# A spectral and gated feed-forward layer on one core: turned token tiles that share tables, six loads in two queues, and new orders

## The chip, the cores and the metric

The kernel runs on one core of a Trainium2 chip. The metric is device time in microseconds (us) of one launch; the lower the better. The engines are named as in the profile: PE (TensorE, matmuls; PEld its weight loads), DVE (VectorE), ACT (ScalarE), POOL (GpSimd) and SP (SyncE, which only issues transfers). Each engine works through its own instructions in order and waits on semaphores for the others. Transfers between DRAM and the on-chip memory (SBUF) run on 16 DMA engines that all issuers share.

## The reference

Two steps on x of 2048 tokens by 576 channels, in bf16: a spectral filter of the normalised input, added to x, and then a gated feed-forward of the normalised sum, added again.

```python
def _A_ref(x, w_r, w_i):
    B, S, D = x.shape
    X = jnp.fft.rfft2(x.astype(jnp.float32), axes=(-2, -1))
    X = X * (w_r + 1j * w_i)
    return jnp.fft.irfft2(X, s=(S, D), axes=(-2, -1)).astype(jnp.bfloat16)

def _B_ref(x, w_gate, w_up, w_down):
    return (_gelu(x @ w_gate) * (x @ w_up)) @ w_down

h = x + _A_ref(_layernorm(x), A_w_r, A_w_i)
h2 = h + _B_ref(_layernorm(h), B_w_gate, B_w_up, B_w_down)
```

The inner width of the feed-forward is 4608; the norms have no weights.

## The kernel before

The transforms are done as matmuls with cosine and sine tables. Token s = 16 n1 + n2 stands in partition n1 of tile n2, so x is 16 tiles of 128 by 576 in one buffer `XO`, and a row of SBUF is a run of 16 x 576 numbers in DRAM.

**Loads** (lines 421 to 464). SP issues all of them, in the order of `LORD` (line 25): `x0-2` is tiles 0 and 1 of x, `a0-4` four tiles of the first table `ATB` (cosines and sines of the token transform, 128 by 128 per tile). Then come the tables `FT` and `BT`, 22 pieces of the spectral weights into `WS`, and the tables of the later stages. Every list of rows starts with 128 partitions, or with 16 blocks of rows for the weights.

**A stage** (lines 470 to 560). The order of its work is written out by hand in `SEQ1` (line 24), a word for each step; each engine sees its own words in that order. The tiles go in six groups of 2, 2, 3, 3, 3 and 3 (`GROUPS`). By word:
- `B` c: the statistics of tile c on DVE, two `bn_stats` (line 480). Tiles 3, 4 and 13 have theirs from ACT: `S` c the sum (line 471), `Q` c the sum of squares (line 475).
- `v` i, `q` i, `c` i: variance on DVE, square root on ACT, reciprocal on DVE for group i.
- `x` i: the group's tables times that factor into `ATS`, on POOL (line 505, `P`) or DVE (line 510, `D`).
- `n` i: the negative of the upper half of the channels into `XN`, on POOL (line 552).
- `M` i: the group's matmuls on PE (line 536). Five passes k per group, in the order 1, 3, 4, 0, 2, each in a PSUM bank of its own: four take 128 channels from each half of the 576, in two matmuls per tile; pass 4 takes the 64 channels left over, as two matmuls with 32 columns.
- `E` n and `F` n: the eviction of pass n (five for each group) from PSUM into `U`, by ACT (`A`) or DVE (`D`), line 547; `F` is the second half of a pass whose `E` did the first.
- `k`: matmuls on zeros, which nothing reads.

POOL's instructions wait for one another: each writes the key `_pool` (line 186).

**Middle stages** (lines 601 to 689). 16 frequency blocks i go through D (matmuls over channels, line 606, evicted to `CUS` by ACT), B (line 616, evicted to `YS`), T (product with the weights, DVE, into `TP`, two buffers), Z (sums, DVE), V (line 646) and R (the leftover frequencies), in the order of `SEQF` (line 28). Then come the last transforms, the second norm and the feed-forward (from line 731 on), whose matmuls fill the rest of the run.

**Stores** (line 978). Each of the 16 tiles leaves in two parts, from SP; the last tile is cut at channel 448.

Of the kernel before, what the change touches and what calls it, by code (L numbers as in the profile page):

```python
# [4 lines left out]
BF16 = mybir.dt.bfloat16  # L5
# [7 lines left out]
NZ = 5  # L13
# [10 lines left out]
SEQ1 = """k14 Q3 B1 B0 n0 S3 n2 v0 B2 v1 q0 q1 c0 x0D M0 S4 c1 Q4 B5 B6 E4A E2A v2 B7 q2 n1 E0A E1A x1P c2 k104 M1 B8 x2P B9 E6A n3 v3 E3A E5A E8A q3 k202 M2 B10 B12 E9A n4 E11A E12A S13 c3 B11 E10A E7A v4 x3P M3 B14 q4 c4 E13A E14A x4P B15 Q13 v5 E17A q5 E16A E15D M4 c5 E19A E20A x5D E18D E23A n5 E22D E21D E24A M5 E25A F23D F24A E26A F25D E27A E29A F29A E28D F28D F22A F26D F27A""".split()  # L24
LORD = "x0-2 x2-4 a0-4 x4-8 a4-8 x8-12 x12-16 a8-16".split()
SPLIT = tuple(int(w[1:-1]) for w in SEQ1 if w[0] == "F")
ACT_TILES = tuple(int(w[1:]) for w in SEQ1 if w[0] == "Q")
SEQF = """w0 w1 D0 D1 D2 B0 T0 D3 B1 Z0 T1 B2 D4 T2 D5 Z1 B3 B4 T3 D6 Z2 w2 D7 Z3 B5 V1 V0 T4 T5 Z4 B6 w3 B7 T6 D8 Z5 T7 V2 D9 Z6 B8 T8 V3 Z7 V4 D10 B9 R0 D11 V5 Z8 B10 T9 R1 T10 B11 D12 Z9 V6 D13 Z10 B12 T11 D14 T12 B13 V8 Z11 V7 B14 T13 Z12 D15 Z13 T14 V9 R2 V10 Z14 B15 V13 T15a T15b V11 Z15a V12 Z15b R3 V14 V15 R4""".split()
# [17 lines left out]
def build_tables():  # L46
# [27 lines left out]
    T["ATAB"] = A.reshape(128, 16 * 128)  # L74
    I = I.reshape(128, 16, 128)
    T["ITAB"] = np.stack([I[:, :NPRE], -I[:, :NPRE]], 1).reshape(128, -1)
# [10 lines left out]
    dr = np.concatenate([np.arange(256, 288), np.arange(544, 576)])  # L87
    for o, kk in enumerate((k2o, k2e)):
        for h, fn in enumerate((np.cos, np.sin)):
            for t in range(2):  # L90
                fr[3 * o + t, :, h] = fn(ang(np.arange(128 * t, 128 * t + 128), kk))
            fr[3 * o + 2, 0:64, h] = fn(ang(dr, kk))
# [5 lines left out]
    for st in range(2):  # L98
        g = 1 - st
        for p in range(128):  # L100
# [31 lines left out]
            for zp, t, cf in terms:  # L132
                V[st, zp, p, t, :, sl, 0] = cf.real
                V[st, zp, p, t, :, sl, 1] = cf.imag
    B[:, 2] = -B[:, 0]
# [177 lines left out]
def _build(nc, A_x, A_w_r, A_w_i, B_w_gate, B_w_up, B_w_down, out):  # L313
# [28 lines left out]
    XN = sb.alloc("XN", [128, NT, 288], BF16)  # L342
# [17 lines left out]
    MK = sb.alloc("MK", [128, 4], F32)  # L360
    OS = sb.alloc("OS", [128, 2, D], BF16)
# [23 lines left out]
    ATB = sb.alloc("ATB", [128, NT, 128], BF16)  # L385
# [6 lines left out]
    TP = sb.alloc("TP", [128, 2, 2, 2, KW], BF16)  # L392
# [25 lines left out]
    P.op(POOL, lambda g: g.memset(MK[:, :], 0.0), w=["MK"])  # L418
    for j in range(4):
        P.op(POOL, lambda g, j=j: g.memset(MK[32 * j:32 * j + 32, j:j + 1], 1.0), w=["MK"])  # L420
    xv = A_x[0].rearrange("(p c) d -> p c d", c=NT)
    ov = out[0].rearrange("(p c) d -> p c d", c=NT)
    tabs = dram["ATAB"].rearrange("p (c k) -> p c k", c=NT)

    def x_load(i, c0, c1):
        P.dma(SP, XO[:, c0:c1, 0:D], xv[:, c0:c1, :], f"x{i}", w=[("X", c) for c in range(c0, c1)])

    def atb_load(i, c0, c1):
        P.dma(SP, ATB[:, c0:c1, :], tabs[:, c0:c1, :], f"atb{i}", w=[("ATB", c) for c in range(c0, c1)])

    for i, w in enumerate(LORD):
        (x_load if w[0] == "x" else atb_load)(i, int(w[1:].split("-")[0]), int(w.split("-")[1]))
# [33 lines left out]
    P.op(POOL, lambda g: g.memset(U[64:128, 4, :, :, :], 0.0), w=["Uz"])  # L466
# [11 lines left out]
    def ln1_tile(c):  # L478
        for h in range(2):
            P.op(DVE, lambda v, c=c, h=h: v.bn_stats(ST1[:, c, h, :], XO[:, c, 288 * h:288 * h + 288]), r=[("X", c)], w=[("ST1", c, h)])  # L480

    def ln1_var(i):
        c0, c1 = GROUPS[i]
        for c in range(c0, c1):
            if c in ACT_TILES:
                P.op(DVE, lambda v, c=c: v.tensor_scalar(TM[:, 0, c:c + 1], SA[:, 0, c:c + 1], SA[:, 0, c:c + 1], 1.0 / (D * D), op0=ALU.mult, op1=ALU.mult), r=[("SA0", c)], w=[("TM", c)])
            else:
                P.op(DVE, lambda v, c=c: v.bn_aggr(MV1[:, c, :], ST1[:, c, :, :]), r=[("ST1", c, 0), ("ST1", c, 1)], w=[("MV1", c)])
        for c in range(c0, c1):
            if c in ACT_TILES:  # L490
                P.op(DVE, lambda v, c=c: v.tensor_scalar(MV1[:, c, 1:2], SA[:, 1, c:c + 1], 1.0 / D, TM[:, 0, c:c + 1], op0=ALU.mult, op1=ALU.subtract), r=[("SA1", c), ("TM", c)], w=[("MV1", c)])
# [10 lines left out]
    def ln1_scale(i, eng):  # L502
        c0, c1 = GROUPS[i]
        if eng == POOL:
            P.op(POOL, lambda g, c0=c0, c1=c1: g.tensor_tensor(ATS[:, c0:c1, :], ATB[:, c0:c1, :],
                                                               RS1[:, c0:c1].unsqueeze(2).to_broadcast([128, c1 - c0, 128]), op=ALU.mult),
                 r=[("RS1", i)] + [("ATB", c) for c in range(c0, c1)], w=[("ATS", c) for c in range(c0, c1)])
        else:
            for c in range(c0, c1):
                P.op(DVE, lambda v, c=c: v.tensor_scalar(ATS[:, c, :], ATB[:, c, :], RS1[:, c:c + 1], None, op0=ALU.mult),  # L510
                     r=[("RS1", i), ("ATB", c)], w=[("ATS", c)])
# [11 lines left out]
    def a_mm(i):  # L523
        c0, c1 = GROUPS[i]
        for k in AORD:
            b = a_bank(i, k)
            for c in range(c0, c1):
                o = 128 * (c - c0)
                if k == 4:
                    parts = [(XO[:, c, 256 + 288 * h:288 + 288 * h], 32 * h, 32 * h + 32, True, True) for h in range(2)]  # L530
                else:
                    d0 = 128 * (k // 2)
                    x2 = XN[:, c, d0:d0 + 128] if k % 2 else XO[:, c, 288 + d0:416 + d0]
                    parts = [(XO[:, c, d0:d0 + 128], 0, 128, True, False), (x2, 0, 128, False, True)]
                for lhs, p0, p1, s, e in parts:
                    P.op(PE, lambda t, b=b, lhs=lhs, p0=p0, p1=p1, s=s, e=e, o=o, c=c: t.matmul(bank(b, p0, p1, o, o + 128), lhs, ATS[:, c, :], start=s, stop=e),  # L536
                         r=[("X", c), ("ATS", c)] + ([("XN", c)] if k % 2 else []), w=[("PS", b)])

    def a_ev(n, eng, late=False):
# [4 lines left out]
        m, b, w = c1 - c0, a_bank(i, k), 64 if k == 4 else 128  # L544
        src = bank(b, 0, w, 0, 128 * m).rearrange("p (n g e) -> p n g e", n=m, g=16)[:, :, g0:g1, :]
        dst = U[0:w, k, g0:g1, c0:c1, :].rearrange("p g n e -> p n g e")
# [3 lines left out]
    def x_neg(i):  # L550
        c0, c1 = GROUPS[i]
        P.op(POOL, lambda g: g.tensor_scalar(XN[:, c0:c1, :], XO[:, c0:c1, 288:D], -1.0, 1.0, op0=ALU.mult, op1=ALU.mult),  # L552
             r=[("X", c) for c in range(c0, c1)], w=[("XN", c) for c in range(c0, c1)])

    ENG = {"A": ACT, "D": DVE, "P": POOL}
    RUN1 = {"k": idle_mm, "S": act_sum, "Q": act_sq, "B": ln1_tile, "v": ln1_var, "q": ln1_sqrt, "c": ln1_rs, "M": a_mm, "x": ln1_scale, "E": a_ev, "F": lambda n, eng: a_ev(n, eng, True), "n": x_neg}
# [15 lines left out]
    P.alias([("XN", c) for c in range(NT)], [("V", g, c) for g in range(NG) for c in range(2)])  # L572
    uk = [[("U", i, k, h) for i in range(len(GROUPS)) for h in range(2)] + (["Uz"] if k == 4 else []) for k in range(5)]
# [27 lines left out]
    def st_D(i, eng=ACT):  # L601
        b0, s3 = FB["D", i], i % 3
        for o in range(2):
            b = b0 + o
            for m, us in enumerate((1 - o, 3 - o, 4) if o == 0 else (4, 1 - o, 3 - o)):
                P.op(PE, lambda t, b=b, m=m, us=us, o=o: t.matmul(bank(b, 0, 128, 0, 2 * HK), U[:, us, i, :, :], FT[:, 3 * o + (2 if us == 4 else us // 2), :], start=(m == 0), stop=(m == 2)),  # L606
                    r=[("U", q, us, i // 8) for q in range(len(GROUPS))] + (["Uz"] if us == 4 else []) + ["FT"], w=[("PS", b)])
        ev(eng, CUS[:, s3, :, :].rearrange("p a (j r) -> p a j r", r=2), banks(b0, 2, 2 * HK).rearrange("p r (a j) -> p a j r", a=2),
           [("PS", b0), ("PS", b0 + 1)], [("CU", s3)])
# [10 lines left out]
    def st_T(i, q0=0, q1=KW, hs=(0, 1)):  # L620
        g, sl = GORD[i], i % 2
# [3 lines left out]
        P.op(DVE, lambda v: v.tensor_tensor(TP[:, sl, :, :, q0:q1], y4, w4, op=ALU.mult),  # L625
             r=[("Y", sl), ("Wn", i)] + (wkeys[0] if 1 <= g < 9 else wkeys[1] if g else wkeys[0] + wkeys[1]), w=[("T", sl, h) for h in hs])
# [6 lines left out]
    def st_Z(i, hs=(0, 1)):  # L633
        sl, z3 = i % 2, i % NZ
# [291 lines left out]
    P.alias([("ATB", c) for c in range(NT)], [("AT", f) for f in gu_early])  # L926
# [13 lines left out]
    fdead = ["DT", "IT", "J0", "J1", "ZD"] + [(n_, c) for n_ in ("ATB", "ATS") for c in range(NT)] + [("G", 0, 0), ("G", 0, 1), ("G", 1, 0), ("G", 1, 1), ("Y", 0), ("Y", 1)]  # L940
    fdead += [("T", a, h) for a in range(2) for h in range(2)] + [("Z", a) for a in range(NZ)] + [("ZR", a, h) for a in range(2) for h in range(4)]
# [21 lines left out]
    def down(tb, p):  # L963
# [3 lines left out]
        for h, (d0, d1) in enumerate(((0, cut), (cut, D))):  # L967
# [10 lines left out]
            P.dma(SP, ov[:, c, d0:d1], OS[:, p % 2, d0:d1], f"so{p % 2}{h}", r=[("OS", p % 2, h)], w=[("OUT", p % 2, h)])  # L978
# [65 lines left out]
```

## Time and profile before

Three runs took 491.40, 491.56 and 491.87 us, median 491.56. The profiled execution took 491.75, of which the span from the first to the last instruction is 490.0.

| stretch, us | what | PE busy | DVE busy | ACT busy | POOL busy | DMA share |
|---|---|---|---|---|---|---|
| 0 to 7.67 | first loads, norms of the first tiles | - | from 3.68 | from 4.43 | - | - |
| 7.67 to 20.37 | rest of the A stage | 10.73 of 12.70 | 12.10 | 11.71 | 8.62 | 1.08 |
| 48.60 to 60.00 | last transforms, second norm | 11.24 of 11.40 | 9.04 | 9.24 | 4.66 | 1.01 |

The granted TensorE clock is 1.00 throughout. A DMA share of 1 means that all 16 engines had a packet all the time; it can pass 1 a little where packets overlap.

The loads that the A stage waits for, by issue and landing:

| piece | KB | issued | landed |
|---|---|---|---|
| x0-2 | 288 | 0.73 | 3.66 |
| x2-4 | 288 | 1.19 | 4.41 |
| a0-4 | 128 | 1.65 | 4.71 |
| x4-8 | 576 | 2.12 | 7.67 |
| a4-8 | 128 | 2.59 | 8.55 |
| x8-12 | 576 | 3.07 | 10.31 |
| x12-16 | 576 | 3.54 | 11.77 |
| a8-16 | 256 | 4.01 | 12.45 |

The groups' matmuls start on PE at 7.29 (M0), 10.30, 11.96, 15.04, 16.78 and 18.50 (M5). The profile's table of groups has each of the 26 `bn_stats` at 0.44 (one starts every 0.36), POOL's `XN` of two tiles at 0.67 and of three at 0.91, its scaled tables of two at 0.61 and of three at 0.83, and ACT's evictions of 128 by 384 at 0.47 to 0.49 (one every 0.37).

### The profile page before, as it was taken

How to read it: one execution, taken by the hardware profiler on the slowest of the kernel's cores; microseconds unless marked ns; L12 is line 12 of the kernel's file. 1: busy time of each engine (PE TensorE's matmuls, PEld its weight loads, DVE VectorE, ACT ScalarE, POOL GpSimd, SP SyncE). 2: the span in 40 equal slices, each digit the busy share in tenths (PEclk: the TensorE clock that was granted, in tenths of full speed). 3: DMA queues.
4: the chain of work that ended last, by engine and by line, in shares of the span. 5: the costliest groups of instructions: out<-in, count | busy, mean ns of one | idle time of the engine just before them, and what ended most of it. 6: DMA issues, size and time to landing. Idle time of an engine off the chain costs nothing.

```text
span 490.0 us, 9967 instructions
## 1 busy us (share of the span) xinstructions
PE 482.7 (99%) x4391; PEld 311.6 (64%) x4392; DVE 193.6 (40%) x397; ACT 151.2 (31%) x297; POOL 31.8 (6%) x58
## 2 busy tenths in 40 slices
PE   7999999999999999999999999999999999999998
PEld 3787788888888744444577644444677544444775
DVE  6799733433576634333311144433211233333111
ACT  6999743223322222322200033233100122323000
POOL 6411441000000020000000000000000000000000
DMA  8990999100001071100000001000000000000000
GB/s 284 248 313 6 354 363 351 30 15 2 1 16 37 18 233 23 26 1 1 2 18 16 17 18 23 17 1 0 7 19 19 7 1 0 1 2 1 13 20 18
DMA packets 25148, 31.20 MB, mean 64 GB/s; under 512 B 11440, under 2 KB 17840, under 8 KB 25104
## 3 DMA queue, kind: packets, MB, share of 16 engines
q1 hardware_dynamic: 22208, 18.62, 13.1%
q0 software_dynamic: 2896, 11.95, 7.0%
q8 instruction: 34, 0.56, 0.5%
q14 instruction: 10, 0.08, 0.1%
HBM read 26.22 MB, written 2.36 MB: 58 GB/s over the span
## 4 chain that ended last, share of the span: by engine, by line
PE 94%; DVE 2%; DMA 1%; issue 1%; POOL 0%; ACT 0%; SPq 0%; DVEq 0%; POOLq 0%
PE PS L872 57%; PE PS L973 29%; PE PS L606 2%; PE PS L536 2%; DMA XO<-in_A_x_dram 1%; PE PS L890 1%; PE PS L616 1%; PE PS L731 1%; DVE TP L625 1%; PE PS L774 1%; PE PS L646 1%; PE PS L908 1%; DVE VR L661 0%; DVE ZS L636 0%; POOL XN L552 0%
## 5 line engine op out<-in xcount | busy, mean ns | idle before, releaser
L872 PE MATMUL PS<-HT,WG 64*128 64x512 bf16 (+1 forms) x2160 | 229.0, 371 | 0.1
L872 PEld LDWEIGHTS PS<-HT,WG 64*128 64x128 bf16 x2160 | 130.3, 94 | 96.9 <-issue 1.1
L881 DVE TENSOR_TENSOR AT<-GL,PS 128x512 bf16<-128x512 bf16 (+1 forms) x147 | 99.3, 676 | 178.3 <-ACT GL L880 178.3
L880 ACT ACTIVATE GL<-PS 128x512 bf16<-128x512 f32 (+1 forms) x147 | 86.5, 588 | 262.9 <-PE PS L872 251.6
L973 PE MATMUL PS<-WD,AT 128*128 128x288 bf16 (+2 forms) x1152 | 144.9, 286 | 0.0
L973 PEld LDWEIGHTS PS<-WD,AT 128*128 128x128 bf16 x1152 | 110.7, 98 | 30.6 <-ACT GL L880 0.8
L872 PE MATMUL PS<-HT,WGX 64*128 64x512 bf16 x486 | 53.4, 376 | 0.0
L976 DVE TENSOR_TENSOR OS<-PS,XO 128x288 bf16<-128x288 f32 (+2 forms) x32 | 14.6, 456 | 94.5 <-PE PS L973 94.4
L872 PEld LDWEIGHTS PS<-HT,WGX 64*128 64x128 bf16 x486 | 23.7, 94 | 28.8
L606 PE MATMUL PS<-FT,U 128*128 128x288 bf16 x96 | 13.7, 286 | 0.0
L625 DVE TENSOR_TENSOR TP<-YS,WS 128x1152 bf16<-128x1152 bf16 (+2 forms) x17 | 11.9, 719 | 2.9 <-ACT YS L598 2.6
L536 PE MATMUL PS<-ATS,XO 128*128 128x128 bf16 (+1 forms) x128 | 10.1, 221 | 2.9 <-ACT U L547 1.2
L895 ACT ACTIVATE EB<-PS 128x288 f32<-128x288 f32 x10 | 4.1, 411 | 27.7 <-PE PS L890 27.7
L480 DVE BATCH_NORM_STATS2 ST<-XO 128x6 f32<-128x288 bf16 x26 | 10.0, 438 | 3.9 <-DMA XO<-in_A_x_dram 3.9
L536 PEld LDWEIGHTS PS<-ATS,XO 128*128 128x128 bf16 (+1 forms) x128 | 7.5, 97 | 5.5 <-DVE ATS L510 1.5
L606 PEld LDWEIGHTS PS<-FT,U 128*128 128x128 bf16 x96 | 9.3, 98 | 2.3
L913 DVE TENSOR_TENSOR XO<-PS,XO 128x576 bf16<-128x576 f32 x10 | 7.6, 757 | 8.0 <-PE PS L908 8.0
L598 ACT ACTIVATE CUS<-PS 128x576 bf16<-128x576 f32 x16 | 10.4, 655 | 0.5 <-PE PS L606 0.2
L598 ACT ACTIVATE YS<-PS 128x576 bf16<-128x576 f32 x16 | 10.1, 655 | 0.0
L547 ACT ACTIVATE U<-PS 128x256 bf16<-128x256 f32 (+5 forms) x29 | 9.7, 391 | 1.0 <-PE PS L536 0.8
L616 PE MATMUL PS<-CUS,BT 128*128 128x288 bf16 x64 | 10.0, 286 | 0.0
L901 DVE TENSOR_TENSOR QB<-PS,EB 128x288 f32<-128x288 f32 x20 | 8.2, 452 | 3.3 <-ACT EB L895 3.3
(79 smaller groups left out, 207.5 us busy)
## 6 DMA issues: line engine op xcount, KB each, us to landing
WD<-in_B_w_down_dram POOLq DMA_DIRECT2D x9, 576.0 KB, 12.2
WG<-in_B_w_up_dram SPq DMA_DIRECT2D x4, 1152.0 KB, 7.5
WG<-in_B_w_gate_dram POOLq DMA_DIRECT2D x4, 1152.0 KB, 9.9
out_dram<-OS SPq DMA_DIRECT2D x30, 72.0 KB, 1.6
XO<-in_A_x_dram SPq DMA_DIRECT2D x3, 576.0 KB, 7.2
WGX<-in_B_w_up_dram SPq DMA_DIRECT2D x1, 1152.0 KB, 6.1
WGX<-in_B_w_gate_dram POOLq DMA_DIRECT2D x1, 1152.0 KB, 9.9
HT<-HN SPq DMA_TRANSPOSE x60, 2.4
```

Source lines behind the costliest of these rows:

```text
L480: P.op(DVE, lambda v, c=c, h=h: v.bn_stats(ST1[:, c, h, :], XO[:, c, 288 * h:288 * h + 288]), r=[("X", c)], w=[("ST1", c, h)])
L536: P.op(PE, lambda t, b=b, lhs=lhs, p0=p0, p1=p1, s=s, e=e, o=o, c=c: t.matmul(bank(b, p0, p1, o, o + 128), lhs, ATS[:, c, :], start=s, sto ...
L547: fn = (lambda v: v.tensor_copy(dst, src)) if eng == DVE else (lambda a: a.activation(dst, src, ACTF.Copy))
L598: fn = (lambda v: v.tensor_copy(dst, src)) if eng == DVE else (lambda a: a.activation(dst, src, ACTF.Copy))
L606: P.op(PE, lambda t, b=b, m=m, us=us, o=o: t.matmul(bank(b, 0, 128, 0, 2 * HK), U[:, us, i, :, :], FT[:, 3 * o + (2 if us == 4 else us // ...
L616: P.op(PE, lambda t, b=b, tb=tb, m=m, s3=s3, sp_=sp_: t.matmul(bank(b, 0, 128, 0, KW), BT[:, sp_, tb, :], CUS[:, s3, m, :], start=(m == 0) ...
L625: P.op(DVE, lambda v: v.tensor_tensor(TP[:, sl, :, :, q0:q1], y4, w4, op=ALU.mult), r=[("Y", sl), ("Wn", i)] + (wkeys[0] if 1 <= g < 9 els ...
L872: op = P.op(PE, lambda t, h0=h0, kt=kt, wt=wt, b=b, s=(not second and j == 0), e=(second and j == n - 1): t.matmul(bank(b, 0, 128, c0, c1) ...
L880: P.op(ACT, lambda a: a.activation(GL[:, s2, c0:c1], bank(b0, 0, 128, c0, c1), ACTF.Gelu_apprx_tanh), r=[("PS", b0)], w=[("GL", s2)])
L881: P.op(DVE, lambda v: v.tensor_tensor(AT[:, f, c0:c1], GL[:, s2, c0:c1], bank(b0 + 1, 0, 128, c0, c1), op=ALU.mult), r=[("GL", s2), ("PS", ...
L973: P.op(PE, lambda t, b=b, d0=d0, d1=d1, f=f, p=p: t.matmul(bank(b, 0, 128, 0, d1 - d0), AT[:, f, 128 * p:128 * p + 128], WD[:, f, d0:d1], ...
L976: P.op(DVE, lambda v, b=b, d0=d0, d1=d1, p=p, c=c: v.tensor_tensor(OS[:, p % 2, d0:d1], bank(b, 0, 128, 0, d1 - d0), XO[:, c, d0:d1], op=A ...
```

## The change

Token s and token 1024 - s have the same cosines and sines up to signs, so tiles n2 and 16 - n2 can share a table when one of them is turned: its rows run backwards in each half of 64 partitions. Seven tiles (13, 14, 15, 9, 10, 11, 12) are turned; 9 table tiles are loaded instead of 16. The tiles now stand in `XO` by position, in the order in which they are loaded: positions 0 to 3 hold tiles 0 to 3, positions 4 to 6 tiles 13 to 15 (turned), 7 to 11 tiles 4 to 8, and 12 to 15 tiles 9 to 12 (turned). All words and groups count positions. The signs are put right by the later tables and by a column `SG` of plus and minus ones, with which ACT scales the `CUS` eviction of the blocks with odd `GORD`.

The loads of x and of the first table are six pieces. Those with `@` are issued by ACT at the head of its queue, the others by SP; `+` and `-` give the direction.

```diff
-LORD = "x0-2 x2-4 a0-4 x4-8 a4-8 x8-12 x12-16 a8-16".split()
+LORD = "x0-4+ a0-4@ x13-16- x4-9+@ a4-9@ x9-13-".split()
+RUNS = [(*(int(v) for v in w[1:-1].split("-")), w[-1] == "-") for w in (v.rstrip("@") for v in LORD) if w[0] == "x"]
+N2 = [n for n0, n1, _ in RUNS for n in range(n0, n1)]
+REV = [r for n0, n1, r in RUNS for _ in range(n0, n1)]
+TAB = [16 - n if r else n for n, r in zip(N2, REV)]
+NTAB = 9
...
+    def rows(ap, c, n, d0, d1):
+        lead = [[S * D // 2, 2], [-NT * D, 64]] if REV[c] else [[NT * D, 128]]
+        return bass.AP(ap.tensor, (63 * NT * REV[c] + N2[c]) * D + d0, [*lead, [1, (n - 1) * D + d1 - d0]])
+
+    def x_load(i, c, n, eng):
+        P.dma(eng, XO[:, c:c + n, 0:D].rearrange("p c d -> p (c d)"), rows(A_x, c, n, 0, D), f"ld{i}", w=[("X", k) for k in range(c, c + n)])
...
-            P.dma(SP, ov[:, c, d0:d1], OS[:, p % 2, d0:d1], f"so{p % 2}{h}", r=[("OS", p % 2, h)], w=[("OUT", p % 2, h)])
+            P.dma(SP, rows(out, c, 1, d0, d1), OS[:, p % 2, d0:d1], f"so{p % 2}{h}", r=[("OS", p % 2, h)], w=[("OUT", p % 2, h)])
```

The orders are written anew. `b` c is now the second half of the statistics of position c, `m` c the squared mean that was part of `v`, on POOL or DVE, and `t` i a copy of 32 channels into a longer `XN`, on POOL.

```diff
-SEQ1 = """k14 Q3 B1 B0 n0 S3 n2 v0 B2 v1 q0 q1 c0 x0D M0 S4 c1 Q4 B5 B6 E4A E2A v2 B7 q2 n1 E0A E1A x1P c2 k104 M1 B8 x2P B9 E6A n3 v3 E3A E5A E8A q3 k202 M2 B10 B12 E9A n4 E11A E12A S13 c3 B11 E10A E7A v4 x3P M3 B14 q4 c4 E13A E14A x4P B15 Q13 v5 E17A q5 E16A E15D M4 c5 E19A E20A x5D E18D E23A n5 E22D E21D E24A M5 E25A F23D F24A E26A F25D E27A E29A F29A E28D F28D F22A F26D F27A""".split()
+SEQ1 = """t1 n0 b1 b0 B0 B1 Q3 b2 S3 v0 n1 m3P B2 b6 q0 n2 S4 c0 t0 b5 x0P k104 v1 m4P B7 B5 B6 k14 b10 M0 q1 c1 Q4 b9 E0A E1A Q13 n3 v2 q2 E2A x1P M1 b7 k202 n4 E4A b8 E5A E3A B9 c2 E7A x2P B8 S13 B11 v3 q3 b11 B10 c3 t3 t2 x3P E6A B12 b12 M2 v4 B14 E8A E10A E9A E11A q4 c4 E14A M3 b14 E13A E12A t4 E15A b15 E17A x4P B15 n5 m13D v5 q5 t5 E16D c5 M4 x5D E18A E19A E20D E23A E24D E21A M5 E25A F23D F27D E27D E28D E26A E22A F24A F25D F26A E29A F22D F29A F27D F28A""".split()
...
-SEQF = """w0 w1 D0 D1 D2 B0 T0 D3 B1 Z0 T1 B2 D4
...
+SEQF = """D0 w0 D2 D1 B0 D3 B1 T0 B2 D5 D4 Z0 T1
```

Pass 4 becomes one matmul of 128 columns per tile (32 channels of the upper half with their sign turned, 32 of the lower half, and 64 columns that meet zeros in `FT`), so `U` needs no zero fill. `x4P` works in two pieces, because its three tables don't follow one another.

```diff
-    P.op(POOL, lambda g: g.memset(U[64:128, 4, :, :, :], 0.0), w=["Uz"])
...
                 if k == 4:
-                    parts = [(XO[:, c, 256 + 288 * h:288 + 288 * h], 32 * h, 32 * h + 32, True, True) for h in range(2)]
+                    parts = [(XN[:, c, 192:320], True, True)]
...
+    def x_tail(i):
+        c0, c1 = GROUPS[i]
+        P.op(POOL, lambda g: g.tensor_scalar(XN[:, c0:c1, 288:320], XO[:, c0:c1, 256:288], 1.0, 1.0, op0=ALU.mult, op1=ALU.mult),
+             r=[("X", c) for c in range(c0, c1)], w=[("XT", c) for c in range(c0, c1)])
...
+        if GORD[i] % 2:
+            P.op(ACT, lambda a: a.activation(dst, src, ACTF.Copy, scale=SG[:, 0:1]), r=[("PS", b0), ("PS", b0 + 1), "SG"], w=[("CU", s3)])
+        else:
+            ev(ACT, dst, src, [("PS", b0), ("PS", b0 + 1)], [("CU", s3)])
...
-    TP = sb.alloc("TP", [128, 2, 2, 2, KW], BF16)
+    TP = sb.alloc("TP", [128, 3, 2, 2, KW], BF16)
```

`TP` has three buffers instead of two. The matmuls, evictions and statistics are otherwise the same in number.

## The prediction

> **What bounds the kernel now.** I read the page's shares first, then the chain of waits in order of time, then busy time in windows, then single DMA issues.
>
> ```profile
> span 490.0 us, 9967 instructions
> ...
> PE 94%; DVE 2%; DMA 1%; issue 1%; POOL 0%; ACT 0%; SPq 0%; DVEq 0%; POOLq 0%
> ```
>
> TensorE's matmuls carry 94% of the chain. Everything the change touches but the output stores lies in the first 48.6 us; from 60 us on PE is busy without a break. So a delay of the front is paid in full at the end. The chain there, as start, length and holder:
>
> ```profile
> 2.12 5.55 DMA XO<-in_A_x_dram
> ...
> 7.74 0.92 POOL XN L552
> ...
> 8.80 0.68 POOL XN L552
> ...
> 9.63 0.62 POOL ATS L505
> ...
> 10.30 1.39 PE PS L536 x20
> ...
> 14.35 0.65 ACT U L547 x2
> ...
> 15.04 5.33 PE PS L536 x90
> 20.38 2.21 PE PS L606 x18
> ```
>
> The reader sees a load (tiles 4 to 7, landing at 7.67), three POOL instructions that stand behind it in POOL's own order, and from 15.04 a PE without gaps: groups M3 to M5 of the A stage (line 536) end at 20.37, where the D stage (line 606) starts. 20.37 is the mark that I move. The windows hold busy time by engine, then clock, DMA share, GB/s:
>
> ```profile
> core 0: us, PE busy (x) PEld busy (x) DVE busy (x) ACT busy (x) POOL busy (x), PEclk, DMA share, GB/s
> ...
> 9.00:12.00 3.00, 2.24 (x25) 1.36 (x25) 3.00 (x15) 2.55 (x11) 2.34 (x4) 1.00 1.03 413
> ...
> 20.37:36.00 15.63, 15.63 (x133) 12.65 (x131) 12.52 (x34) 15.34 (x30) 1.53 (x2) 1.00 0.95 302
> 36.00:48.60 12.60, 12.36 (x105) 9.80 (x102) 12.49 (x29) 12.26 (x24) 0.99 (x2) 1.00 0.04 6
> ...
> 60.00:489.00 429.00, 427.52 (x3866) 270.15 (x3860) 143.87 (x253) 99.27 (x180) 12.11 (x18) 1.00 0.13 39
> ...
> 487.00:488.00 1.00, 0.58 (x11) 0.40 (x8) 0.29 (x1) 0.00 (x0) 0.00 (x0) 1.00 0.34 115
> 488.50:489.50 1.00, 0.00 (x0) 0.00 (x0) 0.00 (x0) 0.00 (x0) 0.00 (x0) 1.00 0.15 33
> ```
>
> Two readings: the 16 DMA engines are full from 9 to 12 us, and one then moves 413/(1.03 x 16) = 25.1 GB/s; and between 20.37 and 48.6 PE and ACT are both about 98% busy, so a new order there has at most 0.6 us of ACT's idle time to win.
>
> **The turned loads.** This part decides. Two of the four x pieces now read DRAM as 2 halves of 64 rows walked backwards, [2][64][n x 576], where every list of the kernel before begins with 128, 64 or 16 rows. How a transfer is dealt out to the engines shows in its small end packets, here for the store of the last tile's first part:
>
> ```profile
> DMA packets 144, 0.11 MB, mean 60 GB/s; under 512 B 16, under 2 KB 144, under 8 KB 144
> ```
>
> 128 rows, and 16 packets under 512 B: one end mark from each of 16 engines, each with its own fixed share of the list. No transfer of this trace begins with a count that 16 doesn't divide, so the price of one that begins with 2 is unknown and has two ends. If the shares are cut from the flat list of rows, it stays at 16 engines. If they are cut from the outermost count, a list of 2 goes to two engines, 64 rows each, and 14 stand by. I take the second: an issue lasts some 0.4 us whether it carries 64 or 128 rows, so the cut is made on the list's counts and not row by row, and the outermost count is the one that has been 16-divisible in every spread transfer. That is inference; I give it 0.82. The Trainium skill ("DMA: Bandwidth & Descriptors", "Why a DMA increments its semaphore by 16 and not by 1") states this as a rule: the number of engines is the largest up to 16 that divides the slowest counts of both sides, which makes it 2 for 2 against 128. By it the sum is the 510.0 below, by sixteen engines 491.2; no run here shows which.
>
> Landing of the last piece by the two-engine end. The first load is the yardstick:
>
> ```profile
> XO<-in_A_x_dram SPq DMA_DIRECT2D x1, 288.0 KB, 2.9
> ```
>
> Issued at 0.73, landed at 3.66; its share of 18 KB per engine takes 0.74 us at 25.1, so data runs as if from 2.92. One of the two engines now carries, in KB: x0-4 36, tables 8 + 10, x4-9 45, x13-16 216, x9-13 288: 603 KB, 24.6 us. The tiles at positions 12 to 15 (x9-13) land at **27.5** instead of 11.8; x13-16 (positions 4 to 6) at 2.92 + (36+8+10+45+216 = 315 KB, 12.9) = 15.8.
>
> What is late next. ACT's new order is E0, E1, **Q13**, q2, E2, ...: Q13 reads position 13, so q2 and every eviction from E2 on stand behind 27.5, though their own data came at 16. From there: Q13 0.69 (line 475's row), q2 0.30, c2 on DVE 0.16 and POOL's x2P 0.83 let M2 start 2.2 us after the landing (n4, 0.91, runs beside). DVE, behind c2, still has 10 bn_stats at a pitch of 0.36, v3 to v5 at 0.35, E16 0.47, c5 0.2 and the first scaled table 0.25: 3.6 + 1.05 + 0.9 = 5.6, plus about 0.9 in which c3 and c4 wait for q3 and q4, which ACT runs behind S13 and evictions at 0.26 to 0.37. M5 starts 1.3 + 5.6 + 0.9 = 7.8 after the landing and lasts 27 matmuls at 0.0573 (30 took 1.72 before) = 1.55: A ends 9.4 after it, at 36.9. **Term: 36.9 - 20.37 = +16.5.** Bounds: +14.5 (landing 26.5, post-work 8.4) to +21 (28.3 us of packets if the weight loads beside them slow each by 15%, and a PE that restarts slowly after 6 us idle: its first idle matmuls came 0.42 us apart, later ones 0.21).
>
> SP's list moves up: FT, BT and 22 weight issues start some 2 us earlier, but on the two engines their shares queue behind 27.5. At 25 GB/s FT and BT are done by 28.5, at the 15 of the weight stage the first weights by 34; D needs FT at 36.9, T0 needs weights at 40.4. Hidden, by 6 us or more.
>
> **The stores.** Tiles 4 to 6 and 12 to 15 are stored the same way. In mid kernel the next user of the buffer comes two tiles (8 us) later: nothing. The last tile is turned: 112 KB over two engines at 115/(0.34 x 16) = 21.1 GB/s takes 2.7 us from 487.16, then 32 KB at 33/(0.15 x 16) = 13.8 takes 1.2: landed at 491.05, before 489.46. **Term: +1.6** (0 with 16 engines).
>
> **The rest,** small beside that. Leftover pass: one 128-wide matmul for two 32-wide, 16 fewer at 0.056 = 0.9 us of PE, already in M5's 1.55; hidden before that. Its tails are six POOL instructions without a row: between 0.19 (NM, 3 elements) and 0.67 (XN, 576); by the slope 0.26 to 0.28, with POOL's gap of 0.15; the 1.81 us memset of U goes. Three SG memsets (0.1 each) come. POOL has waits to spare under the late landing. x0 (0.41) and two m (0.13 each) leave DVE for POOL (0.61, 0.2 each); x4P becomes two (1.0 for 0.83). Seven fewer table tiles, 0.23 MB, are 0.55 us of all engines, but not on the two. Three DMA issues lead ACT's queue at 0.4 to 0.67 each (no row for ACT's): the activation-table load ends at 3.2 to 4.0 rather than 2.0, and Q3's tile lands at about 4.4: hidden. Eight of 16 CUS evictions take their scale from a column: no row; line 765, with such a column as bias, takes 0.77, line 475 without 0.69. Between 0 and 8 x 0.08 = 0.6 on a full ACT; I take 0.3. The new D/B/T/Z/V order and a third TP buffer: between -0.6 (ACT's idle) and +1; I take 0.
>
> **Sum.** On the profiled execution, 491.75 with a span of 490.0: 491.75 + 16.5 + 1.6 + 0.3 = 510.15; the median of the runs is 0.2 lower: **510.0**.
>
> **Rivals.**
> Sixteen engines, about even, 491.2 (chance 0.09). For: 128 rows are there to be cut. Then POOL is the chain: after x13-16 lands at about 7 it runs n2, t0, x0P, m4P, n3, x1P, n4, x2P, 5.3 us and eight gaps of 0.15, so M2 starts at 13.5 where it was 11.96; but M2 to M5 now run close behind one another, 4 x 1.55 + 0.3, and end at 20.0. 491.56 - 0.4.
> Sixteen engines, and the last piece no earlier than before (0.05). At 11.8 Q13 holds q2, c2 and E2 as above; q3 behind S13 comes at 15.0, c3 and x3P put M3 at 16.15 (15.04 before) and A ends at 21.05: 492.3. For: bytes ahead of it are the same, 2.65 MB against 2.62. Against: two queues may fill the gaps.
> The other side: faster (0.04). Two queues keep the engines full from 3 us on at 413 GB/s: 2.65 MB by 9.5, x13-16 by 5.7. POOL's chain then starts 1.3 earlier and decides until A ends at 18.9; with 0.3 from the order: 489.8. Against: it needs the turned lists spread and no stall in the first packets.
> That sharing tables doesn't do what it says: it spares 0.55 us of DMA that PE's chain doesn't wait for; this is inside the first rival.
>
> **How the numbers follow.** Two engines 0.82: 504 to 515.5 by the bounds (+14.5 to +21, tail 1.0 to 1.7, rest -0.6 to +1.5), with 0.02 left outside. The range is that one's, 0.80. A change under about 0.2% (1 us) can't be told from none: faster 0.04 + 0.02 of the even case = 0.06, same 0.07, slower 0.87.
>
> **What would show it.** Right: the issue rows of the two turned x pieces reach landing after 14 and 25 us; DMA share far under 1 from 10 to 27 us; ACT idle before the Square of position 13 until that landing; D starts at 36 to 37; end marks of a turned store fewer than 16. Wrong: turned pieces landing within 12 us, or A ending near 20 us; a tail with the last store under 2 us. If they land late and A still ends early, the queue argument on Q13 is what failed.

## The result and the profile after

The changed kernel takes 514.41 us (median; 513.84 to 515.10), the kernel before 491.56 (491.40 to 491.87): a ratio of 1.0465, 95% interval 1.045 to 1.048. It is slower by 22.9 us where 18.4 were forecast, within the range. The profiled execution took 515.1, its span 513.3.

The page's span and its shares of the chain that ended last:

```profile
span 513.3 us, 9943 instructions
...
PE 91%; DMA 6%; ACT 1%; DVE 1%; SPq 0%; issue 0%; DVEq 0%
```

DMA has gone from 1% of that chain to 6%, some 29 us. The chain of waits at the front (start, length, holder) says which transfer it is:

```profile
1.97 28.50 DMA XO<-in_A_x_dram
...
30.49 0.78 ACT JNK L495 x2
31.26 0.19 ACT RS L515
...
32.81 8.12 PE PS L560 x108
40.93 2.24 PE PS L635 x18
```

One load is open from 1.97 to 30.47: the last piece, x9-13. Behind it come the two halves of a Square (JNK, line 495: Q13), the square root for group 2 (RS), and then groups M2 to M5 in one run of 108 matmuls; the D stage (line 635) starts at 40.93, where the kernel before started it at 20.37. The windows (busy time of PE, PEld, DVE, ACT, POOL; granted clock; DMA share; GB/s) show what the machine did until then:

```profile
9.00:12.00 3.00, 0.00 (x0) 0.00 (x0) 0.00 (x0) 0.00 (x0) 0.00 (x0) 1.00 0.13 52
...
15.00:21.00 6.00, 2.10 (x18) 1.84 (x18) 4.28 (x17) 2.50 (x7) 3.50 (x6) 0.50 0.47 134
21.00:27.00 6.00, 2.10 (x18) 1.84 (x18) 0.00 (x0) 0.00 (x0) 0.05 (x1) 0.78 0.49 125
27.00:31.50 4.50, 0.00 (x0) 0.00 (x0) 0.02 (x1) 1.01 (x4) 0.91 (x1) 0.50 0.63 170
...
36.00:40.93 4.93, 4.93 (x81) 4.91 (x79) 4.05 (x17) 4.52 (x15) 3.08 (x10) 0.89 0.66 178
```

From 9 to 12 us no engine works, and the DMA engines are busy for a share of 0.13, which is two of 16 (0.125); before, the same stretch had 1.03 and 413 GB/s. x13-16 landed at 16.7, and until 21 DVE and POOL work on it. Then DVE, ACT and POOL have nothing to do until 30.5, and PE only the 18 matmuls of M1. The clock column (full speed is 1.00) falls to 0.50 while PE waits; it is at 1.00 again for 3.4 us after M1, and then only from 37.1, late in M2 to M5.

The stores of the last tile, the DMA view of 508.5 to 513.3:

```profile
DMA packets 237, 0.13 MB, mean 28 GB/s; under 512 B 132, under 2 KB 236, under 8 KB 236
```

Of 132 packets under 512 B, 128 are the rows of the second store (256 B each). The other 4 are end marks, two a store where the kernel before had 16. From the issue of the last store to the end of the span it is 4.86 us (508.41 to 513.27), before 1.95 (488.00 to 489.95).

The difference of the two profiled executions, 23.3 us of span, is then: A stage +20.56 (40.93 - 20.37); the middle, from the end of A to the first I matmul, 28.46 (69.39 - 40.93) for 28.29 (48.66 - 20.37), +0.2; the long matmul stretch from there to the last matmul -0.3; tail +2.9.

### The profile page after: what moved, and what is told of

It is laid out like the page before. It is cut to its first block, busy times and chain, and to the rows that moved or that the text cites. A ratio compares the mean times of both kernels' runs of the same rounds, so it can differ in the third digit from the quotient of the medians.

```text
span 513.3 us, 9943 instructions
## 1 busy us (share of the span) xinstructions
PE 486.1 (95%) x4375; PEld 289.9 (56%) x4376; DVE 193.1 (38%) x393; ACT 151.6 (30%) x297; POOL 33.1 (6%) x70
## 3 DMA queue, kind: packets, MB, share of 16 engines
q10 hardware_dynamic: 432, 1.03, 0.6%
## 4 chain that ended last, share of the span: by engine, by line
PE 91%; DMA 6%; ACT 1%; DVE 1%; SPq 0%; issue 0%; DVEq 0%
PE PS L904 55%; PE PS L1005 28%; DMA XO<-in_A_x_dram 6%; PE PS L635 2%; PE PS L560 2%; PE PS L648 1%; PE PS L922 1%; PE PS L763 1%; ACT V L627 1%; PE PS L806 1%; PE PS L678 1%; PE PS L940 0%; PE PS L868 0%; ACT YS L627 0%; DVE TP L657 0%; DVE VR L693 0%
## 5 line engine op out<-in xcount | busy, mean ns | idle before, releaser
L904 PEld LDWEIGHTS PS<-HT,WG 64*128 64x128 bf16 x2160 | 104.7, 94 | 122.2 <-issue 0.7
L904 PEld LDWEIGHTS PS<-HT,WGX 64*128 64x128 bf16 x486 | 23.7, 94 | 28.8
L560 PE MATMUL PS<-ATS,XO 128*128 128x128 bf16 x96 | 11.7, 266 | 11.1 <-POOL ATS L529 11.1
L545 PE MATMUL PS<-ZD 128*128 128x512 bf16 x19 | 7.1, 545 | 10.4 <-ACT U L571 9.0
L560 PEld LDWEIGHTS PS<-ATS,XO 128*128 128x128 bf16 x96 | 9.2, 124 | 12.6 <-POOL ATS L529 12.6
L545 PEld LDWEIGHTS PS<-ZD 128*128 128x128 bf16 x20 | 2.4, 130 | 14.0 <-ACT U L571 8.8
L571 ACT ACTIVATE U<-PS 128x256 bf16<-128x256 f32 (+2 forms) x29 | 9.6, 412 | 1.5 <-PE PS L560 1.4
## 6 DMA issues: line engine op xcount, KB each, us to landing
WG<-in_B_w_gate_dram POOLq DMA_DIRECT2D x4, 1152.0 KB, 10.5
```

The source lines that it names most:

```text
L560: P.op(PE, lambda t, b=b, lhs=lhs, s=s, e=e, o=o, c=c: t.matmul(bank(b, 0, 128, o, o + 128), lhs, ATS[:, c, :], start=s, stop=e), r=[("X", ...
L571: fn = (lambda v: v.tensor_copy(dst, src)) if eng == DVE else (lambda a: a.activation(dst, src, ACTF.Copy))
L904: op = P.op(PE, lambda t, h0=h0, kt=kt, wt=wt, b=b, s=(not second and j == 0), e=(second and j == n - 1): t.matmul(bank(b, 0, 128, c0, c1) ...
```

## The experiments

Theory: a list that begins with a count of 2 is moved by two DMA engines, and all that is late follows from that. The rivals: it is slow to walk DRAM backwards; the new orders, two issuing queues and POOL's added work cost as much; and of the late part, that the landing itself, ACT's order or PE's clock decides. Line numbers differ a little between the kernels, where lines were added.

### The lists read forwards

Three runs read the turned pieces with a positive row step, first as a list of 2, of 8 and of 128 rows, and a fourth does so for the stores too:

```diff
-        lead = [[S * D // 2, 2], [-NT * D, 64]] if REV[c] else [[NT * D, 128]]
+        lead = [[S * D // 2, 2], [NT * D, 64]] ...     # fwd_two, loads only
+        lead = [[S * D // 8, 8], [NT * D, 16]] ...     # fwd_eight, loads only
+        lead = [[NT * D, 128]]                         # fwd_load: loads; fwd_both: stores too
```

> The changed kernel, but the two turned pieces read their rows forwards, still as a list that begins with 2 ([2][64][n x 576], row step positive). The rows of tiles at positions 4 to 6 and 12 to 15 then stand in the wrong partitions, so the output isn't the reference's; bytes, packets and instructions are the same. Theory (the count of the outermost list sets the number of engines): nothing changes, pieces land at 16.7 and 30.5 us, A ends at 40.9, 514.4 +- 1. Rival (walking DRAM backwards is what is slow): both pieces land by 12.5 us, A ends near 21 us, 493 to 496.

> The changed kernel with the two turned pieces read forwards as a list that begins with 8 ([8][16][n x 576]); rows of those tiles misplaced, output not the reference's; stores as in the changed kernel. Theory: eight engines take the two pieces; the busiest carry, in KB, 36 + 18 + 45 + 54 + 72 = 225, that is 9.0 us at 25.1 GB/s, so the last piece lands at about 12 to 14.5 us (30.5 with two engines), A ends at 20.5 to 24, and the tail's +2.9 stays: 494 to 498. Rival (backwards is what is slow, or the lists of 64 and of 16 rows make no difference): as with 128 rows, 493 to 495, or as before the edit, 514.

> The changed kernel with the two turned pieces read forwards as one list of 128 rows; rows of those tiles misplaced, output not the reference's; stores stay turned, on two engines. This gives what the front is worth without the two-engine loads. Theory: last piece lands at 11 to 12.5 us, A ends at 19.5 to 21.5 (20.37 in the kernel before), the tail's +2.9 and the middle's +0.2 stay: 493.5 to 496. Rival (orders, two queues and POOL's added work cost the front as well): A ends at 24 or later, 498 or more.

> Turned loads and turned stores both as lists of 128 rows forwards; output not the reference's (rows of the turned tiles misplaced on the way in, and put back unturned). Theory: 2.5 to 3.2 us under the run with the loads alone, since the stores of the last tile go to 16 engines: 490.5 to 493. Rival (the tail grew for another reason, such as later end marks of any SyncE store): within 0.8 of the run with loads alone.

Measured: fwd_two 496.09 (four runs, 494.86 to 496.97), fwd_eight 495.65, fwd_load 495.95 (two runs each; fwd_load's ratio to before 1.0085, 1.0056 to 1.0114), fwd_both 492.63 (1.0022, 1.0008 to 1.0037). At first sight fwd_two speaks for the rival that backward rows are slow. It doesn't. Read forwards, the halves lie one behind the other at the step of the rows, so [2][64] and [8][16] join into one list of 128 before the transfer is issued: each of these loads has sixteen landing events in the trace, where the turned ones of the changed kernel have two. The three are one kernel, run three times; their issues last 0.41 to 0.44 us each, as 128-row lists did before, where the two turned pieces' lasted 0.72 and 0.83. What they give is the worth of the rest of the change, and how far runs of it lie apart. The chain of fwd_load:

```profile
11.16 0.92 POOL XN L577
...
12.22 0.62 POOL ATS L530
...
12.89 1.67 PE PS L561 x18
...
14.99 3.35 PE PS L561 x54
...
21.61 2.24 PE PS L636 x18
```

With 16 engines x9-13 lands at 10.5 and A ends at 21.6 (19.5 to 21.5 expected), 1.2 later than before. POOL holds M1: the table for group 1 (ATS, line 530) stands behind n3 (XN, line 577), which reads a later piece, in its order. Then M2 to M5 run in 6.6 us without a gap (the line shows the first half of them). So the orders cost about a microsecond, not ten. fwd_both ends A at 21.14, and its tail, from the last output addition to the end, is back: it took 3.3 us less than fwd_load (2.5 to 3.2 expected), 0.5 of them by the earlier end of A. Part of what is left goes with PE's clock. In fwd_both's profile it is at 0.50 from 10.3 to 13.7, after the wait for M0, and of its eight runs the three with a mean clock of 1.00 took 491.9 to 492.4, the two at 0.993 took 493.9 and 494.2. So at full clock the change without its two-engine lists is within about 0.6 us of the kernel before.

### Lists that don't join

The same with a second list that begins one row early, so that it can't join the first:

```diff
+        lead = [[63 * NT * D, 2], [NT * D, 64]] ...    # gap_two
+        lead = [[15 * NT * D, 8], [NT * D, 16]] ...    # gap_eight
```

> The changed kernel with the two turned pieces read forwards in two lists that do not join: [2][64][n x 576], the second half beginning one row early (step of 63 rows of tiles for 64), so that the list can't be taken as one of 128. Rows of those tiles are wrong, the output isn't the reference's; bytes and packets are those of the changed kernel. Theory (a list that begins with 2 goes to two engines): the changed kernel's picture, pieces landing at 16 to 17 and 29 to 31.5 us, A ending at 39.5 to 41.5, 513 to 515.5. Rival (backward rows are what is slow): last piece by 12 us, A ends at 21 to 23, 494.5 to 497.

> The same with lists that begin with 8: [8][16][n x 576], each next list one row early (step of 15 for 16). Output not the reference's. Theory: eight engines; the busiest carry 36 + 18 + 45 + 54 + 72 = 225 KB, 9.0 us at 25.1 GB/s, from 2.9 on: last piece at 12 to 14.5 us; Q13 then lets A end at 21.5 to 24.5: 495 to 499. Rivals: as 128 rows, last piece at 10 to 10.6 and 494.9 to 497 in the runs so far (an overlap, so the landing and the end marks decide, 8 or 16 a piece); as two, 514.

gap_two took 515.19 (one run), within the theory's range and far from the rival's 494.5 to 497. Its chain is that of the changed kernel to within 0.13 us:

```profile
1.96 28.51 DMA XO<-in_A_x_dram
...
41.06 2.24 PE PS L636 x18
```

Forwards or backwards is the same; the first count of the list, as it is issued, decides. The rule of the Trainium skill ("DMA: Bandwidth & Descriptors", "Why a DMA increments its semaphore by 16 and not by 1"), that the number of engines is the largest up to 16 that divides the slowest counts of both sides, agrees: 2 gives a share of 0.13, two end marks and 30.5, 128 gives 10.5. The landing events of x9-13 in the traces show the number itself: two in the changed kernel (29.48 and 30.46) and in gap_two (29.45 and 30.48), eight in gap_eight (18.31 to 18.72), sixteen in fwd_load (9.08 to 10.51), beside one at the issue where they are fewer than sixteen.

gap_eight took 502.28 (one run), outside the 495 to 499 expected. x13-16 landed at 12.3 and x9-13 at 18.7 instead of 12 to 14.5. Two of its windows:

```profile
9.00:12.00 3.00, 0.00 (x0) 0.00 (x0) 0.00 (x0) 0.00 (x0) 0.00 (x0) 1.00 1.08 205
12.00:15.00 3.00, 0.58 (x6) 0.59 (x7) 2.72 (x11) 1.74 (x5) 2.08 (x5) 0.51 1.11 159
```

The share says that all 16 engines are busy, at 159 to 205 GB/s where the kernel before moved 413. The weight lists, behind the x pieces in SP's queue, are already running; x9-13's 128 packets of 4608 B took 416 ns in the mean (311 at least), against 178 when nothing ran beside them. The count sets the number of engines and the order of the landings (two 30.5, eight 18.7, sixteen 10.5), but the forecast had left out what runs beside. That this is what made eight late is likely and was not tried with eight; the next run tries it with two.

### SyncE's list held back

```diff
-    P.dma(SP, FT[...], dram["FTAB"][:, :], "ft", w=["FT"])
+    P.dma(SP, FT[...], dram["FTAB"][:, :], "ft", r=[("X", NT - 1)], w=["FT"])
```

> The changed kernel with one wait added: SyncE issues FT, BT and the weights only when the last turned piece (x9-13) has landed. Theory (the three microseconds by which that piece came later than forecast, 30.5 for 27.5, are its packets running slower beside the weight loads): packets of 4608 B stay at 178 to 190 ns from 16 us on, where they took 181 to 379, and the piece lands at 27.3 to 28.2. The weights then come later by the time SyncE lost: its issues lasted 0.6 to 2.1 us each when crowded, so 0.45 to 0.65 each alone, FT and BT at 30 to 31, first weights at 39 to 42 against T0's need at about 40: 510.5 to 515, and the landing is the verdict, not the time. Rival (the piece is late for its own sake: two engines at work for long run slower, or x13-16 before it is what was late): it lands at 29.5 to 30.8 again.

511.3 us (ratio 1.0396, 1.0365 to 1.0426): faster than the changed kernel by 3.1. Windows from 16 to 26 us, first the changed kernel, then hold_sp:

```profile
16.00:26.00 10.00, 4.21 (x36) 3.68 (x36) 4.28 (x17) 2.50 (x7) 3.55 (x6) 0.63 0.48 131
```

```profile
16.00:26.00 10.00, 4.20 (x36) 3.67 (x36) 3.76 (x16) 1.98 (x7) 3.08 (x6) 0.67 0.13 53
```

Alone, the two engines move x at 53 GB/s, every packet of 4608 B in 178 ns, and the piece lands at 26.6, below even the 27.3 to 28.2 of the theory. In the changed kernel the total was 131 GB/s, most of it weights; 90 of the 128 packets took under 190 ns there too, but the slowest tenth over 321, and the mean was 213 (the expectation's "181 to 379" describes the slow ones, not all). A ends at 36.6. The rest of SP's list, FT to weights, issued from 26.7 on, wasn't missed: PE has no gap at the start of D.

### The order behind the last landing

q13_late puts Q13 and S13 behind E17A in ACT's order; late_all puts everything that reads the last piece behind everything that doesn't:

```diff
# q13_late
- ... E0A E1A Q13 n3 v2 q2 E2A ... x2P B8 S13 B11 v3 q3 ... b15 E17A x4P ...
+ ... E0A E1A n3 v2 q2 E2A ... x2P B8 B11 v3 q3 ... b15 E17A Q13 S13 x4P ...
# late_all
+ ... E0A E1A n3 v2 q2 E2A x1P M1 ... x2P B8 B11 v3 q3 ... x3P E6A M2 ... M3 ... E17A E16D E18A E19A
+     n4 B12 b12 v4 q4 c4 t4 Q13 S13 x4P B14 b14 b15 B15 n5 m13D v5 q5 t5 c5 M4 x5D ...
```

> The changed kernel with Q13 and S13 (ACT's two passes over the tile at position 13) put behind E17A in ACT's order; loads as in the change. Theory (ACT's order around Q13 is what keeps groups M2 and M3 behind the last landing, as the prediction has it): q2 and E2A run at 17 to 19, M2 and M3 start there, and only M4 and M5 are left after 30.5: A ends at 37.5 to 39.5, 511 to 513. Rival (n4 on POOL, which also reads the last piece, stands ahead of x2P and holds M2 just as well): x2P still ends at about 32.2, M2 starts at 32.3, A ends at 40 to 40.7: 513.5 to 514.3.

> Every instruction that reads the last piece (n4 on POOL; B12, b12 and what follows v4 on DVE; q4, Q13, S13 on ACT) put behind all that doesn't need it; loads as in the change. Theory (the landing at 30.5 is the bound, and the order decides only what is left after it): M2 and M3 end by 24, then M4 and M5 alone after the landing; PE idle before them, so at about half clock (0.106 us a matmul): A ends at 38.3 to 39.8, 511.6 to 513.4. Rival (the work after the landing is bound by DVE's and POOL's chain and not by PE's 108 matmuls): A ends at 36 to 37.5, 509.5 to 511. Rival 2 (order does nothing): 514.4.

q13_late took 516.09 (1.0497, 1.0466 to 1.0527), slower than the changed kernel and outside both ranges. A ended at 41.8. POOL in its timeline (start, length, instruction, idle before and its releaser):

```profile
20.39 0.61 POOL L529 TENSOR_TENSOR ATS<-ATB,RS 128x256 bf16<-128x256 bf16 x1
30.25 0.91 POOL L576 TENSOR_SCALAR XN<-XO 128x864 bf16<-128x864 bf16 x1 [9.25 <-DMA XO<-in_A_x_dram]
31.31 0.83 POOL L529 TENSOR_TENSOR ATS<-ATB,RS 128x384 bf16<-128x384 bf16 x1
```

With Q13 gone from ACT's path, c2 was done at 21.0. The table of group 2 (the last line) still ran at 31.3, because n4, which reads the last piece, stands ahead of it on POOL. (The profile's chain puts the table down to a DVE instruction that ended at 31.28, but the table reads nothing of it, and it starts 0.15 after n4, POOL's usual gap.) That is the rival's mechanism. Its price was off too: from 35.3 on, Q13 and S13 stood behind five evictions of M2 and M3, which put the last pass of M4 and all of M5 off until 39.7.

late_all took 511.84 (two runs, 511.07 and 512.62; 1.041, 1.0365 to 1.0455): 2.6 less than the changed kernel. M2 and M3 were done at 25.9, the piece landed at 29.8, M4 and M5 ran from 32.2 to 36.9. The time lies in the first theory's range; A's end (38.3 to 39.8 expected) lies in the rival's, 36 to 37.5, though not for its reason: the 54 matmuls ran in one stretch of 4.70 us, so PE did bind. They took 0.087 each instead of 0.106, since the clock was back at 1.00 from 35.4, before they were done. The landing bounds; the order was worth about 2.5 us by the medians, and 4.0 by the profiled executions, whose landings lie 0.6 apart.

### PE kept at work

```diff
- ... c5 M4 x5D ...
+ ... c5 k429 M4 x5D ...      # late_all with 29 idle matmuls of 512 columns before M4
```

> The run late_all (all that reads the last piece put last; A ended at 36.93, groups M4 and M5, 54 matmuls, took 4.70 us with the granted clock at 0.50 until 35) with 29 idle matmuls of 512 columns put before M4, so that PE works from 26 to 32 us. Theory (the wait halves PE's clock and the matmuls after it pay): the granted clock stays at 1.00 from 26 on, the 54 matmuls run at 0.057 us where their inputs are there; x5D's last table at 34.4 then holds M5, A ends at 35.5 to 36.1, 510.4 to 511.4 against 511.84. Rival (the clock recovers or not whatever PE does; M4 and M5 are slow for their inputs): A ends at 36.6 to 37.2 and the time doesn't fall.

510.53 (two runs, 510.33 and 510.72; 1.038, 1.035 to 1.041). The interval overlaps late_all's, so the time alone doesn't decide here; the trace does. The same windows in late_all and in late_warm:

```profile
26.00:32.00 6.00, 0.00 (x0) 0.00 (x0) 1.78 (x8) 2.21 (x8) 1.62 (x3) 0.71 0.58 170
32.20:36.30 4.10, 4.08 (x46) 3.95 (x47) 2.93 (x14) 1.91 (x7) 2.80 (x9) 0.61 0.66 163
```

```profile
26.00:32.00 6.00, 5.93 (x35) 2.90 (x34) 1.77 (x8) 2.58 (x7) 1.35 (x3) 1.00 0.55 167
32.20:36.30 4.10, 4.10 (x59) 3.40 (x58) 3.70 (x17) 2.89 (x11) 3.03 (x10) 1.00 0.66 167
```

The clock stays at 1.00, and M4 and M5 take 1.66 and 1.78 us instead of 4.70 together. A ends at 36.2, just past the 36.1 expected: the idle matmuls ran 0.5 us too long, and the piece landed 0.3 later than in late_all. So PE's wait costs twice, once as the wait and again in what follows it: 1.3 us in these 54 matmuls, of which A's end kept 0.7.

### The turned pieces through POOL's queue

split2 loads each turned piece by two DMAs from POOL, every second partition each, puts x4-9 last in position so that the last tiles stored are unturned, and holds SP's list back until the turned pieces are in:

```diff
-LORD = "x0-4+ a0-4@ x13-16- x4-9+@ a4-9@ x9-13-".split()
+LORD = "x0-4+ a0-4@ x13-16- x9-13- a4-9@ x4-9+".split()
...
+        for j in range(2):
+            dst = bass.AP(dst.tensor, dst.offset + j * pt, [[2 * pt, 64], [1, n * D]])
+            src = bass.AP(A_x.tensor, ((63 - j) * NT + N2[c]) * D, [[S * D // 2, 2], [-2 * NT * D, 32], [1, n * D]])
+            P.dma(POOL, dst, src, ...)
```

> The changed kernel in a form that computes the reference: each turned piece loaded by two DMAs on POOL's queue (every second partition each, [2][32][n x 576]) instead of one on SyncE's; x13-16 and x9-13 ahead of x4-9 in position, so that the last four tiles stored are unturned; SyncE's FT, BT and weights wait for the two turned pieces; POOL's memsets but two stand behind its four issues. Theory (two engines for one list, and no more, was the price): if POOL's DMAs go to other engines than SyncE's, four engines carry 99 + 108 KB and four 99 + 144 KB at 25.1 GB/s, landings at 11 to 14; A ends 7.5 to 8.6 after the last, at 20 to 22.5; the tail's +2.9 is gone (last store lands 1.5 us after its issue): 491.3 to 494. Rival 1: POOL's DMAs too are dealt to the same two engines: the landings stay at 16 and 26 to 30, A ends near 35 to 37, 506 to 510. Rival 2: the weights, held until the turned pieces have landed, are late for T0: D starts by 23 but the middle (28.5 us) grows by 2 or more: 494.5 to 498.

496.86 (1.0107, 1.009 to 1.0124). The pieces landed at 12.6 and 14.2 (11 to 14 expected), and the last store was no longer late: the span ends 2.4 us after the last output addition starts, 2.3 in the kernel before, 5.2 in the changed kernel. A window and the chain:

```profile
9.00:12.00 3.00, 0.00 (x0) 0.00 (x0) 0.00 (x0) 0.00 (x0) 0.00 (x0) 0.84 0.51 190
```

```profile
2.18 10.40 DMA XO<-in_A_x_dram
...
12.66 0.92 POOL XN L586
...
18.17 0.84 POOL ATS L539
...
19.05 6.66 PE PS L570 x108
25.72 2.24 PE PS L645 x18
```

A share of 0.51 is eight engines for four lists of two: POOL's lists went to four pairs at once, where SP's two shared one pair. The Trainium skill ("DMA: Bandwidth & Descriptors", "Why a DMA increments its semaphore by 16 and not by 1") says so of lists from POOL's queue (consecutive engines from a cursor that goes round, while SP's and ACT's lists take the lowest ones); the share agrees. But A ended at 25.7 instead of 20 to 22.5. The order is still the one made for x13-16 at an early hour: x0P, the table of the first group, waits behind n2 on POOL, and S4 behind the same piece on ACT, so that not even M0 started before 12.6; from there to 19.0 the chain is POOL's (n2, t0, x0P, m4P, n3, x1P, n4, x2P). That was the missed step, not the loads. The middle took 28.5, so the held weights weren't late (rival 2 falls).

split3 sorts the A stage by landing, M0, M1 and M5 first, with idle matmuls in PE's waits:

```diff
+ ... x1P M1 E2A E3A E4A E5A Q13 S13 ... x5D E6A E7A E8A E9A B11 b11 B12 b12 k508 M5 E25A E26A Q4 S4 n2 ...
+     E29A x2P k213 M2 n4 B7 b7 B8 b8 B9 b9 t3 ... x3P k305 M3 t4 ... x4P M4 ...
```

> The run split2 (x13-16 landed 12.6, x9-13 14.2, A ended 25.7, 496.86) with the A stage ordered by landing: groups M0, M1 and M5 (the unturned tiles, landed by 8.7) first, every instruction on x13-16 and x9-13 behind them on ACT, DVE and POOL, Q4 and S4 behind M5's first evictions, idle matmuls in PE's two waits; SyncE's list waits for x13-16 only. Theory (split2's A end is set by its order, in which POOL's x1P and ACT's S4 stand behind x13-16, and then by PE at half clock): M5 done by 13.5, M2 starts at 15.5 to 16.5, M3 at 17.8 to 19, M4 at 19.5 to 20.5; A ends at 21 to 22.5: 492.2 to 494. Rival (what follows the landing is one chain of n, statistics and scaling on POOL and DVE, as long as before whatever stands ahead of it): A ends at 24.5 to 26, 495.5 to 497. Faster than the kernel before (under 490.8) is not expected: its A stage ended at 20.37.

It failed: 503.89 (1.0252, 1.0238 to 1.0267), D started at 31.4. ACT in its timeline:

```profile
13.85 0.66 ACT L581 ACTIVATE U<-PS 128x256 bf16<-128x256 f32 x2
18.25 0.87 ACT L581 ACTIVATE U<-PS 128x384 bf16<-128x384 f32 x2 [3.75 <-PE PS L570]
19.01 0.69 ACT L505 ACTIVATE JNK<-XO 128x576 bf16<-128x576 bf16 x1
```

The eight idle matmuls before M5 need the bank that E9A empties, which ran at 14.2, so they didn't fill a wait: they ran from 14.56 to 17.88 at half clock, ahead of M5. ACT waited for M5 (3.75 us idle), and Q4, whose piece had landed at 12.5, started at 19.0. A second loss came at the end: the last A matmul was done at 28.9, but DVE had seven evictions after it, 2.3 us, before D could start. Neither the theory nor its rival had this. What a well sorted order would bring stays open; no version tried here is faster than the kernel before.

## Why the prediction was right

**The turned loads on two engines.** Right, given 0.82, and shown by gap_two against fwd_load. It holds for the list as it is issued: fwd_two's list of 2, as written, ran on sixteen. The prediction's own reason, that issues last 0.4 us whatever the rows, isn't what shows it: the turned pieces' lasted 0.72 and 0.83. Of the marks named in the prediction, x13-16 landed at 16.7 (15.8 forecast), a turned store has two end marks, the DMA share is 0.13, ACT is idle before Q13 until the landing. Two marks came out otherwise: D started at 40.9, not at 36 to 37, and the share was 0.13 only from 9 to about 12, then 0.47 to 0.7 with the weights beside.

**The range.** By the prediction's own bounds it runs from 506.5 (491.55 + 14.5 + 1.0 - 0.6) to 515.8; the stated 504 is lower without a reason. 514.41 lies in both, near the top, because both large terms were too small.

**The term +16.5** measured +20.56, at the upper bound of +21. It was mis-sized in two places. First, "the tiles at positions 12 to 15 land at 27.5": 30.47. hold_sp shows the cause, SP's later loads beside (FT, BT and the weights). The busier engine's packets took 27.5 us (30.47 - 2.92) where 24.6 were forecast; with SP's list held back they took 23.7 (26.64 - 2.92). So 25.1 GB/s per engine was a little low, and the weights slowed x by 16%, which stood in the bound (15%) and not in the centre. Second, "A ends 9.4 us after it": 10.47. DVE's sum was nearly right: M5's first table was done 8.0 after the landing, at 38.48, where M5's start was forecast at 7.8. But PE was behind: M2 to M5 ran without a gap for 8.12 us at a clock that began at 0.50, so M5 started at 39.26, 0.8 after its table. The bounds named a PE that restarts slowly; late_warm, with M4 and M5 in another order, shows that it is the clock.

**ACT's Q13 holds the queue.** True in the chain, but not alone. "n4 runs beside" was the wrong half of that step: q13_late shows that n4 on POOL holds group 2 to the same moment. Q13 alone gives nothing back; late_all, which moves both and every other reader of the piece, gives about 2.5 us. n4 alone wasn't tried.

**The stores, +1.6:** measured +2.9. Against the last matmul, the last end mark came 2.5 later (512.00 - 20.40 for 489.09); the rest is SP, which went on 0.79 after that mark where it took 0.38 before. The term, bounded at 1.0 to 1.7, had the packets too short by 0.9 and nothing for the wait. fwd_both shows the whole term to hang on the two engines.

**The rest, +0.3:** the middle grew by 0.2, with the eight CUS evictions that take a scale column at 0.73 to 0.75 us for 0.65. The first rival, sixteen engines and POOL as the chain, was right in what it named: fwd_load and fwd_both show POOL's order holding M1. Its A end of 20.0 was measured as 21.1, its 491.2 as 492.6 (fwd_both). **SP's weights hidden by 6 us or more:** they were hidden, though SP's FT issue alone lasted 9.5 us, which no step foresaw.

## What to carry to other kernels

Before a load or store is turned around or cut, look at the first count of its list: with 2 there, two of 16 engines did the work (53 GB/s for 413 here), and no order behind it won back more than 4 us of the 23. When a piece lands late, ask of every engine's queue what stands behind its first reader, not only of the one in the chain: here ACT and POOL both held the same group. And a forecast of a landing needs the traffic beside it: it added 3.8 us to a landing at 26.6 with two engines, and with eight, where its part wasn't measured, the piece came at 18.7 for 12 to 14.5.

## What was not expected of the hardware

SP was stopped by lists that it had only to issue. Behind the two turned pieces, its issue of FT lasted 9.5 us, and the next nine 1.1 to 2.1 each; in hold_sp the same ten took 0.33 to 0.61. What stops it wasn't tried; in gap_eight FT's issue lasted 0.52, and the stop (up to 2.4 us) came at the seventh weight list. In the changed kernel's timeline:

```profile
2.83 9.54 SPq L231 DMA_DIRECT2D FT<-c_ftab  x1
```

Packets slow down far more than the bytes beside them suggest: 4608 B took 178 ns alone and 416 ns in the mean with the weights' short packets beside them (gap_eight), where the sum was 159 to 205 GB/s, against 413 in the kernel before. Whether memory, the write side or the engines' own sharing sets this wasn't tried. In the changed kernel PE stopped at 7.9, and its clock was halved at 13.2. It came back only after 3 to 5 us of matmuls: they start again at 32.2 in three runs, and the clock is 1.00 from 35.2 in q13_late, 35.4 in late_all and 37.3 in gap_two. The Trainium skill ("TensorE: Matmul & The Clock Gate", "Part 1: The HAM clock gate (the "warmup" mystery)") gives half rate for an idle PE and some 3.4 us of sustained work to full rate; the rows agree on the half rate, and show 3.0 to 5.2 us for the other.
